# Decay tables made at once, two products on VectorE and a later copy out of PSUM in a fused RWKV and expert-routing kernel

## The chip, the core and the metric

The kernel runs on one core of a Trainium2 chip. A core has five engines with instruction queues of their own: TensorE (PE in the profile; its weight loads are PEld), VectorE (DVE), ScalarE (ACT), GpSimd (POOL) and SyncE (SP), which here only issues DMAs. The metric is the device time of one execution in microseconds. Before the change three runs took 467.05, 468.96 and 474.75 us, median 468.96. Less is better.

## The reference, cut to what matters

```python
# attention: B, H, S, D = 4, 8, 768, 48; everything float32
for t in range(S):
    cur = einsum('bhd,bhe->bhde', u[None] * kt, vt)
    y[:, :, t] = einsum('bhd,bhde->bhe', rt, state + cur)
    state = w[None, :, :, None] * state + einsum('bhd,bhe->bhde', kt, vt)
# bridge: x = y as (B*S, H*D) = (3072, 384) rows
logits = x @ w_gate                       # 8 experts
probs = softmax(logits); expert_idx = argmax(logits)
for e in range(8):                        # F = 1024
    out[mask_e] = gate_w * (relu(x[mask_e] @ w1[e]) @ w2[e])
```

Each head has a decay `w` per channel. In chunks of 128 steps the recurrence becomes matrix products: scores within a chunk (with powers of the decay on both sides, masked to the past), the step's own term r·(u k) on the diagonal, and a state of 48x48 carried from chunk to chunk.

## The kernel before, in words

The attention is cut into 16 units: 4 batches times 4 pairs of heads. The two heads of a pair lie at partitions 0 and 64. A unit has 6 chunks (G) of 128 steps. The loop over `i` (line 509) makes one turn per unit, and one more. Within a turn the program text sets the order on every engine: nothing is reordered, and each engine runs its own queue in that order. Semaphores between engines follow from which tiles an instruction reads and writes; for a PSUM tile they hold by bank, whichever columns are meant.

In a turn i:

- SP issues the load of r and k of unit i+3 (`load_rk`), and near the end that of v and the keys (`load_vk`).
- PE multiplies r·k by u (`p_own`, L258) into the PSUM tile `dsb`. DVE transposes that into `own` (`own_t`, L262). The L258 matmuls are the first of a turn, so their times mark where turns begin.
- PE makes the scores of chunks 0 to 3 into `X0` and `X1` (`p_scores`, L270, 16 passes of the profile), and later those of chunks 4 and 5 into `X23` (L270 again, 8 passes): "the last scores".
- DVE scales r and k of the next unit by the decay table TT (`scale`, L239). POOL waits for `own` by a copy of one element (`turn`, L518), then makes the next unit's r·k (`pairs`, L245) and its decayed keys (`keys`, L249). In four turns `keys` is on DVE.
- ACT writes 12 diagonal blocks of `A` from `own` (`diag`, L276). DVE then copies the masked scores over them: `mask(i, 0)` and `mask(i, 1)` (L282) from X0 and X1, and `mask(i, 2)` (L284), the third mask, from X23.
- PE makes the chunk states into `dsb` (`p_ds`, L293), and DVE scans over them (`scan`, L298).
- PE turns the output of unit i-2 into rows by token (`p_tr`, L331): four chunks into the PSUM tile `tr` and two into `X23`, at columns of the same banks that the last scores use. ACT copies both into the row store `xb` (`keep`, L336 and L337): "the copy of the stored rows".
- PE makes the output of unit i-1 (`p_out`, L313 from A and v, L318 from the state) into `yps`, and ACT copies it out (`out_t`, L323).

Every fourth turn DVE chooses experts for a batch (`choose`), PE ranks the tokens (`p_rank`), and POOL sends rows to DRAM by indirect DMA (`send`, L383). The first units need the tables. `decays(h, n)` (L140 to L144) makes TT for n pairs of heads from pair h on, by one copy and seven doublings; `key_decay` and `p_key_decay` (L147, L152, L153) make the key table T3 by a product on DVE, a transpose on PE and a copy on ACT. Before the loop this is done for pair 0, and in turns 0, 1 and 2 for pairs 1, 2 and 3. `p_fill` (L104) are matmuls whose result nobody reads.

After the loop come nine passes over the experts (`Pass`, L431 for the first layer and L442 for the second). The first pass loads its rows (`first.load`) once the sends of batches 0 to 2 are in DRAM, and transposes them on DVE (`xT`, L423).

Of the kernel before, what the change touches and what calls it, by code (L numbers as in the profile page):

```python
# [21 lines left out]
HP = H // 2  # L22
# [15 lines left out]
def bc(ap, shape):  # L38
    return ap.to_broadcast(shape)


def straight(tc, rk, vk, w, w1, w2, out, flag):
# [8 lines left out]
    nc = tc.nc  # L51
# [33 lines left out]
    def load_rk(i):  # L85
        if i < U:
            b, hp = divmod(i, HP)
            nc.sync.dma_start(rks[i % 3][0:KP], rk[b, hp].rearrange("h p u s -> (h p) u s")[0:KP])
# [12 lines left out]
    def p_fill(n):  # L101

        for _ in range(n):
            nc.tensor.matmul(tr[:, 384:512], lhsT=ident, rhs=ident, start=True, stop=True, skip_group_check=True)  # L104
# [7 lines left out]
        nc.sync.dma_start(rows.rearrange("(e n) c -> e (n c)", e=E)[:, PAD * HP * Q:CAP * HP * Q].rearrange(  # L112
            "e (p z) -> p e z", p=128), bc(zt[:, None, :], [128, E, nz]))

    p_fill(14)
    strict = cp.tile([128, C], FP32, name="strict")
    nc.gpsimd.memset(strict, 1.0)
    nc.gpsimd.affine_select(out=strict, in_=strict, pattern=[[1, C]], base=-1, channel_multiplier=-1,
# [14 lines left out]
    def two(h0, nh, first, second, n):  # L133

        a = TTf[:, h0 * 2 * C + first:h0 * 2 * C + first + n]
        return bass.AP(a.tensor, a.offset, [list(a.ap[0]), [2 * C, nh], [second - first, 2], [1, n]])

    def decays(h0, nh):

        nc.vector.tensor_copy(two(h0, nh, 0, 2 * C - 1, 1), bc(inv[:, h0:h0 + nh, None, None], [KP, nh, 2, 1]))  # L140
        for l in range(7):
            n = 1 << l
            nc.vector.tensor_tensor(two(h0, nh, n, 2 * C - 2 * n, n), two(h0, nh, 0, 2 * C - n, n),  # L143
                                    bc(pw[:, l, h0:h0 + nh, None, None], [KP, nh, 2, n]), op=ALU.mult)  # L144

    def key_decay(h0, nh):
        nc.vector.tensor_tensor(T3c[:, h0:h0 + nh, :], TT[:, h0:h0 + nh, 1, :],  # L147
                                bc(pw[:, 7, h0:h0 + nh, None], [KP, nh, C]), op=ALU.mult)

    def p_key_decay(h0, nh):  # L150
        for hp in range(h0, h0 + nh):
            nc.tensor.transpose(tr[:, hp * 128:hp * 128 + KP], T3c[:, hp, :], ident[0:KP, 0:KP])  # L152
        nc.scalar.copy(T3[:, h0:h0 + nh].rearrange("p a (h d) -> p a h d", h=2),  # L153
                       tr[:, h0 * 128:(h0 + nh) * 128].rearrange("p (a h d) -> p a h d", a=nh, h=2)[:, :, :, 0:D])
# [18 lines left out]
    turn = cp.tile([1, 1], FP32, name="turn")  # L173

    def selection():
        for par in range(2):
            for h in range(2):
                o = 64 * (h ^ par)
                nc.gpsimd.tensor_copy(sel[:, par, :, h * D:(h + 1) * D], bc(ident[0:KP, None, o:o + D], [KP, HP, D]))
        nc.gpsimd.tensor_copy(sel[:, :, :, 2 * D:], wgs)  # L180
# [42 lines left out]
    own = [ca.tile([128, G, 32], FP32, name=f"own{i}") for i in range(2)]  # L223
# [13 lines left out]
    def scale(i):  # L237
        hp, x = i % HP, rks[i % 3]
        nc.vector.tensor_tensor(RKs[i % 3][0:KP].rearrange("p u (c t) -> p u c t", t=C),  # L239
                                x[0:KP].rearrange("p u (c t) -> p u c t", t=C),  # L240
                                bc(TT[:, hp, :, None, :], [KP, 2, G, C]), op=ALU.mult)

    def pairs(i, eng=None):
        x = rks[i % 3]
        (eng or nc.gpsimd).tensor_tensor(rps[i % 2][0:KP], x[0:KP, 0], x[0:KP, 1], op=ALU.mult)  # L245

    def keys(i, eng=None):
        hp, v = i % HP, vks[i % 4]
        (eng or nc.gpsimd).tensor_tensor(Kds[i % 2], v[:, G:2 * G - 1, :], bc(T3[:, hp, None, :], [128, G - 1, 2 * D]),  # L249
                                         op=ALU.mult)  # L250

    def p_own(i):


        hp = i % HP
        x = rps[i % 2][0:KP].rearrange("p (c a j) -> p a c j", a=4, j=32)
        for a in range(4):
            nc.tensor.matmul(dsb[32 * a:32 * a + 2, 240:240 + 32 * G].rearrange("p (c j) -> p c j", j=32),  # L258
                             lhsT=ubs[:, hp, :], rhs=x[:, a], start=True, stop=True, skip_group_check=True)

    def own_t(i):
        nc.vector.transpose(own[i % 2].rearrange("p c m -> p (c m)"), dsb[:, 240:240 + 32 * G])  # L262

    def p_scores(i, cs):
        r = RKs[i % 3]
        for c in cs:
            for h in range(2):
                q = slice(64 * h, 64 * h + D)
                o = X01[h][:, c, :] if c < 4 else X23[:, h, (c - 4) * C:(c - 3) * C]
                nc.tensor.matmul(o, lhsT=r[q, 1, c * C:(c + 1) * C], rhs=r[q, 0, c * C:(c + 1) * C],  # L270
                                 start=True, stop=True, skip_group_check=True)

    def diag(i):
        A = Aw[i % 2]
        for c, h in [(c, 0) for c in range(4)] + [(c, 1) for c in range(4)] + [(c, h) for h in range(2) for c in (4, 5)]:
            nc.scalar.activation(A[:, place(c, h), :], ident, func=ACT.Copy, scale=own[i % 2][:, c, h:h + 1])  # L276

    def mask(i, k):
        A = Aw[i % 2]
        m = strict.bitcast(I32)  # L280
        if k < 2:
            nc.vector.copy_predicated(A[:, 4 * k:4 * k + 4, :], bc(m[:, None, :], [128, 4, C]), X01[k])  # L282
        else:
            nc.vector.copy_predicated(A[:, 8:12, :].rearrange("p (h c) t -> p h c t", h=2),  # L284
                                      bc(m[:, None, None, :], [128, 2, 2, C]),
                                      X23[:, :, 0:2 * C].rearrange("p h (c t) -> p h c t", c=2))

    def p_ds(i):
        v = vks[i % 4]
        d = dsb[:, 0:240].rearrange("p (e g) -> p e g", g=G - 1)  # L290
        for c in range(G - 1):
            for h in range(2):
                nc.tensor.matmul(d[64 * h:64 * h + D, :, c], lhsT=Kds[i % 2][:, c, h * D:(h + 1) * D],  # L293
                                 rhs=v[:, c, h * D:(h + 1) * D], start=True, stop=True, skip_group_check=True)
# [26 lines left out]
    def out_t(i):  # L321
        for k in range(2):
            nc.scalar.copy(yTs[i % 3][0:KP, k], yps[0:KP, k, 0:S // 2])  # L323
# [10 lines left out]
    def keep(i):  # L334
        b, hp = divmod(i, HP)
        nc.scalar.copy(xbs[b % 2][:, 0:4, hp, :], trv[0])  # L336
        nc.scalar.copy(xbs[b % 2][:, 4:G, hp, :], trv[1])  # L337
# [158 lines left out]
        for k, cs in enumerate(((0,), (1, 2), (3, 4), (5,)) if b < B - 2 else ((0, 1), (2, 3, 4, 5))):  # L496
            sends[4 * b + 6 + k] = (b, cs)

    decays(0, 1)
    scale(0)  # L500
    pairs(0, nc.vector)
    key_decay(0, 1)
# [2 lines left out]
    p_own(0)  # L505
    own_t(0)
    p_key_decay(0, 1)
    keys(0)
    for i in range(U + 1):
        last = i == U  # L510
        b, k = divmod(i - 6, 4)
        rt = i >= 6 and k == 0 and b < B - 1
        load_rk(i + 3)
        if not last:
            if i > 0:
                p_own(i)
                own_t(i)
            nc.gpsimd.tensor_copy(turn, own[i % 2][0:1, 0, 0:1])  # L518
            p_scores(i, range(4) if i > 0 else range(2, 4))
            if 0 < i < 3:  # L520
                p_fill(4)
        if i + 1 < U:
            if i + 1 < HP:
                decays(i + 1, 1)
            scale(i + 1)
            if i + 1 < HP:
                key_decay(i + 1, 1)
                p_key_decay(i + 1, 1)
            pairs(i + 1)
            keys(i + 1, nc.vector if i in (7, 8, 11, 12) else None)  # L530
        if i == 0:
            selection()
        if i == 2:
            numbers()
        if not last:
            diag(i)
            mask(i, 0)
            mask(i, 1)
            p_ds(i)
        if rt:  # L540
            p_rank(b)
            slots(b)
        if not last:
            scan(i)
        if 2 <= i:
            p_tr(i - 2)
            keep(i - 2)
        if not last:
            p_scores(i, range(4, G))
            mask(i, 2)  # L550
        if rt:
            gates(b)
            total(b)
            ids(b)
        if i in sends:
            send(*sends[i])
        if 1 <= i:
            p_out(i - 1)
            out_t(i - 1)
        if i % 4 == 1 and i > 4:  # L560
            choose((i - 5) // 4)
        load_vk(i + 3)
        if i == 3:
            clear()
        if i in (12, 13):
            (weights1, weights2)[i - 12](0)
        if i == 14:
            weights1(1)
        if i == U - 1:
            count(cnt3)  # L570
            nc.vector.tensor_scalar(out=viol[:, 12:13], in0=cnt3[:, 0:1], scalar1=float(EARLY), scalar2=None, op0=ALU.is_lt)
            weights2(1, range(2))
            first.load()
            weights2(1, range(2, DT))
# [583 lines left out]
```

## Time and profile before

| | us |
|---|---|
| median of three runs | 468.96 |
| the profiled execution | 470.53 |
| its span, first to last instruction | 468.6 |
| loop over the units, from its first turn but one to the first expert matmul | 21.6 to 185.8 |
| mean of turns 3 to 14 | 10.0 |
| PE busy, share of the span | 421.4, 90% |

A row of the timeline has the start in us, the time from the start of its first to the end of its last instruction, the engine, the line, what is written from what, how many instructions are merged in the row, and in brackets how long the engine was idle before it and what ended that. PE rows count passes: a float32 matmul has two. "Granted clock" is TensorE's, as a share of 2.4 GHz, so 0.50 is 1.2 GHz.

### The profile page before, as it was taken

To read this page: it belongs to the slowest core of one execution; us is meant where nothing else is said; L and a number is where in the kernel's file an instruction comes from. 1 tells how busy PE (TensorE), PEld (TensorE's weight loads), DVE (VectorE), ACT (ScalarE), POOL (GpSimd) and SP (SyncE) were. 2 spreads that over 40 slices of the span, in tenths; PEclk is the share of its full clock that TensorE was granted. 3 is DMA by queue.
4 is the path that set the end of the run, shared out by engine and by line. 5 is a ranking of instruction groups with operands and counts; after the bars stand their busy time and mean duration, and the time that the engine had idled before them with its cause. 6 is when DMAs were issued, how large, how long until landed. Compare 5 with 4: busy or idle time off the path is not lost.

```text
span 468.6 us, 7143 instructions
## 1 busy us (share of the span) xinstructions
PE 421.4 (90%) x2767; PEld 290.9 (62%) x2767; DVE 147.6 (31%) x304; ACT 119.3 (25%) x337; POOL 189.7 (40%) x200
## 2 busy tenths in 40 slices
PE   7386898889788888999999999999999999999992
PEld 6265677668666767877575555555555555455692
DVE  7766445564654642212111111120130120211020
ACT  1334444564644553302202012011011021001200
POOL 3424433465665561133221037046055064076741
PEclk9557757876888888999999999999999999999998
DMA  8902373463445954058584255354273273312401
GB/s 229 254 8 99 107 216 107 139 224 128 149 130 177 375 235 138 18 150 208 148 227 117 84 160 160 93 157 131 90 180 113 90 201 103 104 55 64 139 19 43
DMA packets 33675, 65.22 MB, mean 139 GB/s; under 512 B 17911, under 2 KB 18947, under 8 KB 33632
## 3 DMA queue, kind: packets, MB, share of 16 engines
q1 hardware_dynamic: 28896, 54.83, 40.1%
q0 software_dynamic: 4736, 9.84, 6.2%
q8 instruction: 24, 0.39, 0.4%
q14 instruction: 19, 0.16, 0.1%
HBM read 53.55 MB, written 11.50 MB: 139 GB/s over the span
## 4 chain that ended last, share of the span: by engine, by line
PE 79%; ACT 12%; DVE 3%; issue 1%; POOL 0%; POOLq 0%; DVEq 0%; ACTq 0%
PE X L431 29%; PE yps L442 18%; ACT A L276 9%; PE dsb L442 9%; PE yps L313 8%; PE yps L318 4%; PE X L270 4%; PE dsb L258 2%; DVE TT L143 1%; PE tr L331 1%; PE yps L463 1%; PE dsb L463 1%; ACT xb L336 1%; PE dsb L293 1%; DVE own L262 1%
## 5 line engine op out<-in xcount | busy, mean ns | idle before, releaser
L482 POOL DMA_INDIRECT out_dram<-yo,ix x96 | 94.1, 980 | 158.3 <-DVE yo L479 110.4
L431 PE MATMUL X<-xT,w1s 128*128 128x416 f32 (+2 forms) x432 | 136.2, 475 | 1.3 <-PE yps L442 0.9
L431 PEld LDWEIGHTS X<-xT,w1s 128*128 128x128 f32 x432 | 79.1, 190 | 55.9 <-issue 52.4
L433 ACT ACTIVATE hT<-X 128x416 f32<-128x416 f32 (+2 forms) x72 | 34.5, 479 | 218.9 <-PE X L431 205.8
L442 PE MATMUL yps<-hT,w2s 128*128 128x416 f32 (+2 forms) x288 | 85.8, 451 | 0.7 <-DVE yq L444 0.7
L442 PEld LDWEIGHTS yps<-hT,w2s 128*128 128x128 f32 x288 | 51.4, 190 | 33.0 <-issue 30.9
L276 ACT ACTIVATE A<-ident,own 128x128 f32<-128x128 f32 x192 | 57.9, 388 | 2.8 <-DVE own L262 2.4
L270 PE MATMUL X<-RK 48*128 48x128 f32 x384 | 35.9, 327 | 21.0 <-ACT xb L337 19.8
L444 DVE STREAM_TRANSPOSE yq<-yps 128x416 f32<-128x416 f32 (+2 forms) x18 | 9.7, 537 | 127.8 <-PE yps L442 127.8
L270 PEld LDWEIGHTS X<-RK 48*128 48x128 f32 x384 | 28.6, 218 | 30.7 <-ACT xb L337 22.5
L518 POOL COPY turn<-own 1x1 f32<-1x1 f32 x16 | 21.7, 1359 | 58.2 <-DVE own L262 49.8
L442 PE MATMUL dsb<-hT,w2s 128*128 128x416 f32 (+2 forms) x144 | 42.8, 450 | 0.0
L313 PE MATMUL yps<-A,vk 128*48 128x128 f32 x384 | 37.7, 371 | 0.0
L442 PEld LDWEIGHTS dsb<-hT,w2s 128*128 128x128 f32 x144 | 25.7, 190 | 15.7 <-issue 15.3
L313 PEld LDWEIGHTS yps<-A,vk 128*48 128x48 f32 x384 | 31.0, 168 | 2.6 <-issue 0.9
L383 POOL DMA_INDIRECT rows<-xb,slot x24 | 24.1, 1004 | 20.1 <-DVE osum L379 12.0
L323 ACT COPY yT<-yps 112x384 f32<-112x384 f32 x32 | 13.8, 482 | 67.8 <-PE yps L318 67.8
L423 DVE STREAM_TRANSPOSE xT<-xs 128x416 f32<-128x416 f32 (+2 forms) x27 | 13.1, 535 | 49.0 <-DMA xs<-rows 49.0
L239 DVE TENSOR_TENSOR RK<-rk,TT 112x1536 f32<-112x1536 f32 x16 | 27.6, 1727 | 0.5 <-DMA rk<-in_rk_dram 0.4
L245 POOL TENSOR_TENSOR rp<-rk 112x768 f32<-112x768 f32 x15 | 27.1, 1808 | 0.0
L282 DVE COPY_PREDICATED A<-strict,X 128x512 f32<-128x512 int32 x32 | 23.1, 736 | 10.9 <-ACT A L276 8.8
L249 POOL TENSOR_TENSOR Kd<-vk,T 128x480 f32<-128x480 f32 x12 | 14.3, 1196 | 17.6 <-ACT T L153 17.6
(104 smaller groups left out, 287.5 us busy)
## 6 DMA issues: line engine op xcount, KB each, us to landing
w1s<-in_w_dram SPq DMA_DIRECT2D x40, 384.0 KB, 3.3
w2s<-in_w_dram SPq DMA_DIRECT2D x24, 512.0 KB, 3.5
rk<-in_rk_dram SPq DMA_DIRECT2D x16, 672.0 KB, 5.9
vk<-in_vk_dram SPq DMA_DIRECT2D x16, 528.0 KB, 4.4
xs<-rows SPq DMA_DIRECT2D x28, 169.0 KB, 4.2
out_dram<-yo,ix POOLq DMA_INDIRECT x96, 2.9
rows<-zt SPq DMA_DIRECT2D x1, 1248.0 KB, 7.8
xs<-rows SPq DMA_DIRECT2D x4, 104.0 KB, 2.6
```

The lines of the kernel that those rows point to most:

```text
L239: nc.vector.tensor_tensor(RKs[i % 3][0:KP].rearrange("p u (c t) -> p u c t", t=C), x[0:KP].rearrange("p u (c t) -> p u c t", t=C), bc(TT[: ...
L245: (eng or nc.gpsimd).tensor_tensor(rps[i % 2][0:KP], x[0:KP, 0], x[0:KP, 1], op=ALU.mult)
L270: nc.tensor.matmul(o, lhsT=r[q, 1, c * C:(c + 1) * C], rhs=r[q, 0, c * C:(c + 1) * C], start=True, stop=True, skip_group_check=True)
L276: nc.scalar.activation(A[:, place(c, h), :], ident, func=ACT.Copy, scale=own[i % 2][:, c, h:h + 1])
L282: nc.vector.copy_predicated(A[:, 4 * k:4 * k + 4, :], bc(m[:, None, :], [128, 4, C]), X01[k])
L313: nc.tensor.matmul(o(c, h), lhsT=v[:, c, h * D:(h + 1) * D], rhs=A[:, place(c, h), :], start=c < 2, stop=c == 0, skip_group_check=True)
L383: s_ = nc.gpsimd.indirect_dma_start(out=rows[:, :], out_offset=bass.IndirectOffsetOnAxis(ap=slot[b % 2][:, c:c + 1], axis=0), in_=xbs[b % ...
L431: nc.tensor.matmul(p[:, 0:self.n], lhsT=w1s[self.e % 2][f // 2][:, m, f % 2 * 128:(f % 2 + 1) * 128], rhs=self.t[:, m, 0:self.n], start=m ...
L433: nc.scalar.activation(h[:, f, 0:self.n], p[:, 0:self.n], func=ACT.Relu)
L442: nc.tensor.matmul(p[:, 0:n], lhsT=w2s[self.e % 2][m][:, f, :], rhs=self.h[:, f, 0:n], start=f == 0, stop=f == FT - 1, skip_group_check=True)
L482: s_ = nc.gpsimd.indirect_dma_start(out=out4[:, :], out_offset=bass.IndirectOffsetOnAxis(ap=ix[:, k:k + 1], axis=0), in_=yo[:, k, :], in_o ...
L518: nc.gpsimd.tensor_copy(turn, own[i % 2][0:1, 0, 0:1])
```

## The change

- All four decay tables are made at once ahead of the loop (`decays(0, HP)`), and the key tables of pairs 1 to 3 together in turn 0. Turns 1 and 2 have none of it any more.
- The first unit's `keys` and the second unit's `pairs` run on DVE and no longer on POOL. POOL's one-element copy `turn` is left out in turn 0.
- 17 instead of 14 unread matmuls stand at the start, and the 4 each in turns 1 and 2 are gone.
- In each turn `keep(i-2)` stands behind the last scores and the third mask.
- `numbers` (13 small POOL instructions and two of DVE) moves from turn 2 to 3, and `clear` (zeros for part of the row store) from turn 3 to 4.

```diff
-    p_fill(14)
+    p_fill(17)
...
-    decays(0, 1)
+    decays(0, HP)
     scale(0)
     pairs(0, nc.vector)
     key_decay(0, 1)
...
     p_key_decay(0, 1)
-    keys(0)
     for i in range(U + 1):
...
                 p_own(i)
                 own_t(i)
-            nc.gpsimd.tensor_copy(turn, own[i % 2][0:1, 0, 0:1])
+                nc.gpsimd.tensor_copy(turn, own[i % 2][0:1, 0, 0:1])
             p_scores(i, range(4) if i > 0 else range(2, 4))
-            if 0 < i < 3:
-                p_fill(4)
+        if i == 0:
+            keys(0, nc.vector)
         if i + 1 < U:
-            if i + 1 < HP:
-                decays(i + 1, 1)
             scale(i + 1)
-            if i + 1 < HP:
-                key_decay(i + 1, 1)
-                p_key_decay(i + 1, 1)
-            pairs(i + 1)
-            keys(i + 1, nc.vector if i in (7, 8, 11, 12) else None)
-        if i == 0:
-            selection()
-        if i == 2:
+            if i > 0:
+                pairs(i + 1)
+                keys(i + 1, nc.vector if i in (7, 8, 11, 12) else None)
+            else:
+                pairs(1, nc.vector)
+                key_decay(1, HP - 1)
+                p_key_decay(1, HP - 1)
+                keys(1)
+                selection()
+        if i == 3:
             numbers()
...
         if 2 <= i:
             p_tr(i - 2)
-            keep(i - 2)
         if not last:
             p_scores(i, range(4, G))
             mask(i, 2)
+        if 2 <= i:
+            keep(i - 2)
...
-        if i == 3:
+        if i == 4:
             clear()
```

How the queues stand is shown at three places. First PE in turn 2, from the stored rows of unit 0 (L331) to the outputs of unit 1 (L313, L318) and the next turn's L258; X_69 is X23, and the words in brackets are the engines that an instruction waits for. Before:

```order
L331 MATMUL tr<-sel,yT_179 128x104 [waits Activation_49]
L331 MATMUL tr<-sel,yT_179 128x104 x3
L331 MATMUL X_69<-sel,yT_179 128x104 x2
L270 MATMUL X_69<-RK_168 128x128 [waits Activation_49]
L270 MATMUL X_69<-RK_168 128x128 x3
L313 MATMUL yps<-A_174,vk_85 48x128 x12
L318 MATMUL yps<-RK_167,S_176 48x128 x10
L258 MATMUL dsb<-rp_170,wug 2x192 [waits DVE_49,Pool_49]
```

And with the change:

```order
L331 MATMUL tr<-sel,yT_182 128x104 [waits Activation_49] x2
L331 MATMUL tr<-sel,yT_182 128x104 x2
L331 MATMUL X_69<-sel,yT_182 128x104 x2
L270 MATMUL X_69<-RK_171 128x128 x4
L313 MATMUL yps<-A_177,vk_85 48x128 x12
L318 MATMUL yps<-RK_170,S_179 48x128 x10
L258 MATMUL dsb<-rp_173,wug 2x192 [waits DVE_49,Pool_49]
```

The order of the matmuls is the same; the wait of the last scores for ACT is gone.

Second ACT in turn 2 and at the start of turn 3: the diagonal blocks (L276), the copy of the stored rows (L336, L337) and the copy of an output (L323). Before:

```order
L276 ACTIVATE A_173<-ident,own_177 128x128 [waits DVE_49,Activation_49]
L276 ACTIVATE A_173<-ident,own_177 128x128 [waits Activation_49] x11
L336 COPY xb_182<-tr 128x4x104 [waits PE_49]
L337 COPY xb_182<-X_69 128x2x104 [waits PE_49]
L323 COPY yT_180<-yps 112x384 [waits PE_49]
```

And with the change:

```order
L276 ACTIVATE A_176<-ident,own_180 128x128 [waits DVE_49,Activation_49]
L276 ACTIVATE A_176<-ident,own_180 128x128 [waits Activation_49] x11
L336 COPY xb_185<-tr 128x4x104 [waits PE_49]
L337 COPY xb_185<-X_69 128x2x104 [waits DVE_49]
L323 COPY yT_183<-yps 112x384 [waits PE_49]
```

ACT's order is the same; its second copy (L337) waits for DVE's third mask and no longer for PE alone.

Third DVE from the first transpose of `own` on, in turn 0. Before:

```order
L262 STREAM_TRANSPOSE own_177<-dsb 128x192 [waits PE_49]
L140 COPY TT<-inv 112x2
L143 TENSOR_TENSOR TT<-TT,pw 112x2 [waits DVE_49]
L143 TENSOR_TENSOR TT<-TT,pw 112x2x2 [waits DVE_49]
L143 TENSOR_TENSOR TT<-TT,pw 112x2x4 [waits DVE_49]
L143 TENSOR_TENSOR TT<-TT,pw 112x2x8 [waits DVE_49]
L143 TENSOR_TENSOR TT<-TT,pw 112x2x16 [waits DVE_49]
L143 TENSOR_TENSOR TT<-TT,pw 112x2x32 [waits DVE_49]
L143 TENSOR_TENSOR TT<-TT,pw 112x128 [waits DVE_49]
L239 TENSOR_TENSOR RK_167<-rk_82,TT 112x1536 [waits DMAHW3_49,DVE_49]
L147 TENSOR_TENSOR T3c<-TT,pw 112x128
```

And with the change:

```order
L262 STREAM_TRANSPOSE own_180<-dsb 128x192 [waits PE_49]
L249 TENSOR_TENSOR Kd_174<-vk_84,T_133 128x480 [waits DMAHW2_49,Activation_49]
L239 TENSOR_TENSOR RK_170<-rk_82,TT 112x1536 [waits DMAHW3_49]
L245 TENSOR_TENSOR rp_173<-rk_82 112x768
L147 TENSOR_TENSOR T3c<-TT,pw 112x384
```

The eight table instructions are replaced by `keys(0)` and, behind the scaling, `pairs(1)`; the product for T3 is three times as wide.

## Rows read from the trace of the kernel before

**Rows 1.** The page: PE's busy us and share, and its granted clock in 40 slices.

```profile
PE 421.4 (90%) x2767; PEld 290.9 (62%) x2767; DVE 147.6 (31%) x304; ACT 119.3 (25%) x337; POOL 189.7 (40%) x200
PEclk9557757876888888999999999999999999999998
```

**Rows 2.** The page's costliest groups: busy us, mean ns | idle before, what ended it.

```profile
L270 PE MATMUL X<-RK 48*128 48x128 f32 x384 | 35.9, 327 | 21.0 <-ACT xb L337 19.8
...
L282 DVE COPY_PREDICATED A<-strict,X 128x512 f32<-128x512 int32 x32 | 23.1, 736 | 10.9 <-ACT A L276 8.8
```

**Rows 3.** The timeline, from turn 12's last scores to those of turn 13.

```profile
148.81 0.71 PE L270 MATMUL X<-RK 48*128 48x128 f32 x8 [1.65 <-ACT xb L337]
...
151.74 0.51 PE L258 MATMUL dsb<-rp,wug 112*2 112x192 f32 x8
...
152.38 0.38 DVE L262 STREAM_TRANSPOSE own<-dsb 128x192 f32<-128x192 f32 x1 [1.99 <-PE dsb L258]
...
152.86 3.62 ACT L276 ACTIVATE A<-ident,own 128x128 f32<-128x128 f32 x12 [0.15 <-DVE own L262]
...
154.83 0.61 PE L331 MATMUL X<-sel,yT 112*128 112x104 f32 x4
...
155.97 0.64 DVE L298 TENSOR_TENSOR_SCAN S<-dec,dsb 112x240 f32<-112x240 f32 x1
...
156.78 0.32 ACT L337 COPY xb<-X 128x208 f32<-128x208 f32 x1
157.15 0.80 PE L270 MATMUL X<-RK 48*128 48x128 f32 x8 [1.71 <-ACT xb L337]
```

**Rows 4.** Stretches: length, busy us by engine, then granted clock, DMA share, GB/s.

```profile
57.00:60.80 3.80, 3.80 (x52) 3.05 (x52) 0.73 (x1) 0.00 (x0) 0.52 (x2) 0.72 0.10 14
61.00:72.00 11.00, 10.58 (x92) 8.75 (x88) 4.72 (x6) 5.32 (x16) 4.49 (x3) 0.50 0.73 222
...
144.50:157.00 12.50, 9.29 (x151) 7.81 (x148) 8.63 (x11) 9.23 (x30) 10.01 (x7) 1.00 0.67 222
```

**Rows 5.** The timeline, PE in turn 4 and the start of turn 5.

```profile
60.89 0.82 PE L258 MATMUL dsb<-rp,wug 112*2 112x192 f32 x8
...
64.62 2.04 PE L331 MATMUL tr<-sel,yT 112*128 112x104 f32 x8
...
67.94 1.23 PE L270 MATMUL X<-RK 48*128 48x128 f32 x8 [0.42 <-ACT xb L337]
...
72.84 0.51 PE L258 MATMUL dsb<-rp,wug 112*2 112x192 f32 x8
```

**Rows 6.** The timeline: where turns 1, 2, 3 and 15 begin.

```profile
21.59 0.82 PE L258 MATMUL dsb<-rp,wug 112*2 112x192 f32 x8 [1.93 <-DVE S L298]
...
34.87 0.51 PE L258 MATMUL dsb<-rp,wug 112*2 112x192 f32 x8
...
51.38 0.71 PE L258 MATMUL dsb<-rp,wug 112*2 112x192 f32 x8
...
171.51 0.51 PE L258 MATMUL dsb<-rp,wug 112*2 112x192 f32 x8
```

**Rows 7.** The timeline of the start: DVE's table products, scaling and r·k.

```profile
4.59 2.09 DVE L143 TENSOR_TENSOR TT<-TT,pw 112x2 f32<-112x2 f32 x7
7.05 1.76 DVE L239 TENSOR_TENSOR RK<-rk,TT 112x1536 f32<-112x1536 f32 x1 [0.37 <-DMA rk<-in_rk_dram]
8.73 0.95 DVE L245 TENSOR_TENSOR rp<-rk 112x768 f32<-112x768 f32 x1
...
10.78 4.19 DVE L143 TENSOR_TENSOR TT<-TT,pw 112x2 f32<-112x2 f32 x7
```

**Rows 8.** The timeline from turn 14's last small DVE instruction to the first expert.

```profile
169.29 0.17 DVE L379 TENSOR_TENSOR osum<-osp,osum 128x8 bf16<-128x8 f32 x1
...
184.30 1.10 DVE L423 STREAM_TRANSPOSE xT<-xs 128x256 f32<-128x256 f32 x3 [2.47 <-DMA xs<-rows]
...
185.84 1.56 PE L431 MATMUL X<-xT,w1s 128*128 128x256 f32 x6
```

## The prediction, on record before the run

> **What bounds the kernel now.** I read the page first. PE is busy for 90% of the span, but its granted clock is at full only from the middle on; in the first 40% of the slices it swings between 5 and 9 tenths [rows 1]. So the experts, in the later part of the span, run at the full level of 2.4 GHz, and the turns over the units do not. The groups then say what PE waits for in the turns: of 21.0 us of idle time ahead of the score matmuls, 19.8 ended with ACT's second copy of the stored rows, L337 [rows 2].
>
> The timeline shows why [rows 3]. Turn 13 begins at 151.74. DVE has `own` ready 1.02 later, ACT writes 12 diagonal blocks from 152.86 to 156.48, then makes the two copies, the second until 157.10. Meanwhile PE has gone gapless through L258, L270, L293 and L331 until 155.44, and stands 1.71 us until that copy is done, since the last scores go to its bank. The copy needs nothing from the diagonal; it only stands behind it in ACT's queue. So the chain of such a turn is L258, `own`, 3.62 of diagonal, 0.62 of copies, last scores, outputs, and ACT is the longer half of it.
>
> The clock is the second part of the price. At 57.00 PE starts again after such a wait, and over the next 3.8 us, all of them busy, the clock falls (0.72 on average); from 61 to 72 it is 0.50, which is 1.2 GHz, through PE's whole turn 4 [rows 4]. That turn takes 11.95 us, of which only 0.42 are that wait [rows 5]. Between 144.5 and 157.0 the clock held at 1.00 [rows 4], and there one piece of PE's work, from the last scores at 148.81 to the end of the stored rows at 155.44, holds each group of a turn once without a gap: **6.63 us** [rows 3]. Turns 3 to 14 take 120.13 us together, 10.01 each [rows 6]. They are a mixture of shorter turns with the long wait and of turns near 12 at the low clock.
>
> **The change part by part.** All of it is summed against the profiled execution, 470.53, which lies 1.57 above the median of 468.96.
>
> *Later copy, turns 3 to 14.* The last scores no longer wait for ACT. PE then has the 6.63 of one turn ahead of it, if all it needs comes in time. Measured from a turn's start [rows 3]: the scan ends at 4.87, the diagonal at 4.74, the third mask (0.74, [rows 2]) at about 5.6, the copy behind it at about 6.2, all by 6.63, when the next turn begins. The output's copy on ACT then starts at 6.63 and the next diagonal at 6.63 + 1.12. So PE is the bound, gapless. In three turns the ranking, and in three the choice of experts ahead of `own`, add some 0.2 each (my estimate): 12 x 6.63 + 1.2 = 80.8, against 120.13: **-39.3**. Here I take the clock to stay at full when PE has no gap. The bounds for a turn are 6.63 and 11.53 ([rows 5] without the wait); I take the lower one because the clock held for 12.5 us with one wait of 1.65 in it [rows 3, 4], and where it fell a gap stood before.
>
> The copy's new wait is no accident of this kernel. In the trace matmuls into X23 wait for a read of other columns of the same banks [rows 2]. The Trainium skill (PSUM — Partial Sum Buffer, "PSUM bank collisions raise a hardware error") demands it: two engines are to be kept apart by bank, two readers too. By that rule the wait is not deleted but moved from PE to ACT, behind DVE's third mask; its price is the 0.7 us that stands above in the times of a turn, and it is nil for PE as long as ACT's turn is shorter than PE's.
>
> *Turn 2*, with tables before: 51.38 - 34.87 = 16.51 [rows 6]; now as the others if the clock has risen in turn 1: 6.63, **-9.9**. If not, 11.53 and -5.0.
>
> *Turn 1*: 13.28 [rows 6]. It has no stored rows yet, and I expect it at the low clock, since PE still waits in turn 0. Turn 4 [rows 5] without L331 and the wait (64.62 to 67.94) takes 11.95 - 3.32 = 8.63; L318 at the end of that turn was at full clock already, so about 9.07: **-4.2**. The unread matmuls that go from turns 1 and 2 stood beside the tables, and cost nothing now or then.
>
> *Start.* Between the first `own` and the second unit's scaling, DVE spent 4.38 on tables (0.19 of copy and gaps, 4.19 for seven products, [rows 7]): gone. New on the way to the first diagonal: wider tables ahead of everything, 762 elements more at 1.15 ns (1536 in 1.76, [rows 7]), 0.8 to 0.9, of which 0.37 is covered by DVE's wait for the first r and k: 0.45; `keys(0)` on DVE, 0.6 (480 elements, by the 768 in 0.95 [rows 7]); its wait for T3, 0.2; `pairs(1)` 0.9; T3's product three times as wide, 0.3; two more transposes at the low clock and a wider copy, about 1.0 (estimates). Sum **-1.0**; the bounds are 0 and -2. The three more unread matmuls at the start end before the first scores can begin. `numbers` and `clear` move to turns where POOL and SP have room: nothing.
>
> *End.* Here the gain is partly given back. In the profile 16.0 us pass from the end of turn 14's last small instruction (169.46) to the transposed rows of the first expert (185.40): sends on POOL, then the load. That chain does not shrink with PE. In a short turn the small instruction ends about 7.0 after turn 14's start, so the first expert starts near 23.0; turn 15 begins at 6.8, so 16.2 are left from there, against 185.84 - 171.51 = 14.33 [rows 6, 8]: +1.9. PE has less than two turns of work in those 16.2 (one turn of unit 15, then rows and outputs only), so it stands some 4 to 5 us, and the clock will fall. What that costs the first expert is between 0 and the 7 us that its first layer takes; I take 2.2. **+4.1**.
>
> Sum: -39.3 - 9.9 - 4.2 - 1.0 + 4.1 = -50.3. 470.53 - 50.3 = 420.2, or 418.7 seen from the median. Forecast **419 us**.
>
> **The rivals.**
>
> *The clock still falls in part.* No row shows a whole turn without a gap, so that it holds is inferred. For this rival: from 61 to 72 PE was busy 10.58 of 11.00 and the clock stayed down [rows 4], so eleven us of nearly gapless work can leave it low. Against: no row before shows a fall without a gap ahead of it. If every other turn were at 11.5, twelve turns cost 6 x 4.9 = 29 more: 448.
>
> *Another engine becomes the bound.* ACT's turn is 3.62 of diagonal, 0.62 of copies, the new wait of 0.7 and the output's copies, which I take at under 1: near 5.9. What could lengthen it is DVE and POOL, which stop each other: in the start the seven table products took 4.19 beside two products of POOL, and the same seven 2.09 earlier, beside a short copy [rows 7]. If in short turns POOL's work reaches into the next scaling and holds it for as much as these differ, about 2, the scan ends at 6.9, the third mask at 7.7 and ACT's second copy at 8.1; the output's copy and the next diagonal queue behind it, a turn settles near 7.5, and 12 x 0.9 = 11 more: 430. The Trainium skill (SBUF — State Buffer, "SBUF: two separate sides") states this as a lock held for a whole instruction, against VectorE instructions with two SBUF inputs; the two prices of the products agree with it.
>
> *The last scores wait anyway*, for the third mask of the turn before or the stored rows' bank. Against: PE's order list has no wait there. Only the start and turns 1 and 2 would gain, 1.0 + 4.2 + 6.5 (turn 2 at the mean of 10.0): 457.
>
> *Slower: the clock never rises.* The place is the end of turn 1. Before, gaps and bursts alternated, and the clock came back with the outputs of some turns. If gapless turns at 1.2 GHz leave it there, as 61 to 72 did for eleven us, turn 1 ends at 29.7 and 13 turns of 11.53 bring turn 15 to 179.5 instead of 171.51: +8, and PE at the low level then needs 19 instead of 14.3 to the first expert (11.53, 3.3 of stored rows [rows 5], and about 4.2 of outputs): +5. That is 482. It decides from 10.0 us per turn upward.
>
> **How the numbers follow.** Chances: forecast 0.70, clock falls in part 0.17, another engine 0.06, waits anyway 0.03, slower 0.04. The forecast's own bounds: turn 2 at the low clock (+5) or one late turn more upward, no loss of clock at the end and a start 1 us better downward: 412 to 428. The range reaches up to the second rival and to the milder half of the first, a fall in every third turn at most: **408 to 440**. A measurement of this kernel tells about 2% from no change. Faster by over 2% (below 459.6) are the forecast and the first two rivals: 0.93. Within 2%, where 457 may be read: 0.03. Slower: 0.04.
>
> **What would show it.** In the new profile: no idle time ahead of L270 ended by L337; L258 rows 6.6 to 6.9 apart from turn 2 or 3 on, and a granted clock of 1.00 over them; L337 waiting for L284 on ACT; turn 1 at 20 to 21; a wait of DVE for the first expert's rows of 4 us or more longer than 2.47, PE idle there, and the clock low behind it. L258 rows over 9 apart with the clock at 0.50 would make the forecast wrong by the first or last rival; 7.3 or more apart at full clock, with PE waiting for DVE or ACT, by the second.

## The result, and the profile after

The changed kernel takes **421.38 us** (median of 4 runs, 420.53 to 422.24) against 468.91 (4 runs, 467.05 to 474.75) on the same chip: a ratio of **0.900**, 95% interval 0.896 to 0.903. The forecast was 419 us, the range 408 to 440. The profiled execution takes 422.24, with a span of 420.4 against 468.6, so 48.2 us are to be found.

The page, PE's busy time and its granted clock, to be held against [rows 1]; then three groups with the idle time ahead of them, PE's score matmuls, PE's L258 and ACT's second copy, to be held against [rows 2]:

```profile
PE 393.9 (94%) x2757; PEld 270.7 (64%) x2757; DVE 141.8 (34%) x280; ACT 119.8 (28%) x335; POOL 188.7 (45%) x197
PEclk9679599999999899999999999999999999999997
```

```profile
L270 PE MATMUL X<-RK 48*128 48x128 f32 x384 | 33.2, 309 | 1.3 <-DVE RK L239 1.3
L258 PE MATMUL dsb<-rp,wug 112*2 112x192 f32 x128 | 8.5, 339 | 3.7 <-DVE S L298 3.5 <-DVE rp L245 0.2
L337 ACT COPY xb<-X 128x208 f32<-128x208 f32 x16 | 5.3, 332 | 13.5 <-DVE A L284 11.7 <-DMA rows<-xb,slot 1.7
```

The 19.8 us in which PE waited for ACT's copy are gone. ACT itself now waits 11.7 us ahead of L337, for DVE's third mask: the wait has moved, and PE does not see it. Between the start and the last slice the granted clock falls in two places: in the slice with the 8, from 137 us on, behind the wait for the first expert's rows, which was foreseen, and in the slice with the 5, around 42 to 53 us, which was not.

The timeline of turn 8, one of the undisturbed ones (columns as in [rows 3]):

```profile
73.98 0.51 PE L258 MATMUL dsb<-rp,wug 112*2 112x192 f32 x8
...
75.10 3.62 ACT L276 ACTIVATE A<-ident,own 128x128 f32<-128x128 f32 x12
...
77.61 0.71 PE L270 MATMUL X<-RK 48*128 48x128 f32 x8
...
78.93 0.74 DVE L284 COPY_PREDICATED A<-strict,X 128x512 f32<-128x512 int32 x1
79.70 0.33 ACT L337 COPY xb<-X 128x208 f32<-128x208 f32 x1 [0.59 <-DVE A L284]
79.70 0.90 PE L318 MATMUL yps<-RK,S 48*48 48x128 f32 x20
```

The last scores start at 77.61, while ACT is still busy with its diagonal, and the copy comes 2 us behind them. The next L258 row is at 80.53, 6.55 after this turn began.

Now the exception, turns 3 and 4, first as timeline rows, then as stretches (columns as in [rows 4]):

```profile
34.82 0.51 PE L258 MATMUL dsb<-rp,wug 112*2 112x192 f32 x8
...
35.78 1.72 DVE L239 TENSOR_TENSOR RK<-rk,TT 112x1536 f32<-112x1536 f32 x1
...
37.41 3.45 DVE L198 TENSOR_SCALAR le<-wug 112x4 f32<-112x4 f32 x1
37.49 1.80 POOL L245 TENSOR_TENSOR rp<-rk 112x768 f32<-112x768 f32 x1
...
39.26 1.19 POOL L249 TENSOR_TENSOR Kd<-vk,T 128x480 f32<-128x480 f32 x1
...
40.41 0.28 POOL L183 CAST tri<-strict 128x128 bf16<-128x128 f32 x1
...
40.64 0.19 POOL L184 MEMSET ones<- 128x128 bf16 x1
...
40.98 1.33 DVE L282 COPY_PREDICATED A<-strict,X 128x512 f32<-128x512 int32 x2
...
42.20 0.63 DVE L298 TENSOR_TENSOR_SCAN S<-dec,dsb 112x240 f32<-112x240 f32 x1
...
42.98 0.51 PE L258 MATMUL dsb<-rp,wug 112*2 112x192 f32 x8 [1.54 <-DVE S L298]
```

```profile
43.00:54.00 11.00, 11.00 (x108) 9.23 (x108) 5.22 (x7) 5.32 (x17) 4.93 (x5) 0.55 0.29 78
54.10:120.10 66.00, 66.00 (x1103) 55.39 (x1101) 55.09 (x101) 52.19 (x163) 54.79 (x41) 1.00 0.83 273
131.40:136.70 5.30, 0.00 (x0) 0.00 (x0) 0.43 (x2) 0.86 (x2) 0.00 (x0) 0.95 0.63 169
136.80:141.40 4.60, 4.23 (x18) 3.52 (x18) 0.56 (x2) 1.16 (x3) 0.00 (x0) 0.70 0.02 8
```

`numbers` ends with two instructions of DVE on 112x4 elements. The first, L198, takes 3.45 us. It starts with POOL's r.k product, goes on through its keys, and ends when POOL has come to a memset. The two masks and the scan stand behind it in DVE's queue, PE's next L258 waits for that scan, and after 1.54 us of idle PE the clock is at 0.55 through the whole of turn 4, although PE is busy in every moment of it. From 54.10 to 120.10 PE then has no gap, and the clock no fall.

The end, against [rows 8]: DVE waits for the first expert's rows, PE behind it. In the last two of the stretches above PE is idle for 5.30 us, and behind that the clock is at 0.70.

```profile
113.45 0.51 PE L258 MATMUL dsb<-rp,wug 112*2 112x192 f32 x8
...
120.18 0.51 PE L258 MATMUL dsb<-rp,wug 112*2 112x192 f32 x8
...
136.27 1.10 DVE L423 STREAM_TRANSPOSE xT<-xs 128x256 f32<-128x256 f32 x3 [8.96 <-DMA xs<-rows]
136.77 2.21 PEld L431 LDWEIGHTS X<-xT,w1s 128*128 128x128 f32 x6 [5.59 <-DVE xT L423]
136.77 2.92 PE L431 MATMUL X<-xT,w1s 128*128 128x256 f32 x6 [5.38 <-DVE xT L423]
```

### The profile page after: what moved, and what is told of

Same layout as the page of the kernel before. It is cut to its first block, busy times and chain, and to the rows that moved or that the text cites. A ratio compares the mean times of both kernels' runs of the same rounds, so it can differ in the third digit from the quotient of the medians.

```text
span 420.4 us, 7088 instructions
## 1 busy us (share of the span) xinstructions
PE 393.9 (94%) x2757; PEld 270.7 (64%) x2757; DVE 141.8 (34%) x280; ACT 119.8 (28%) x335; POOL 188.7 (45%) x197
## 4 chain that ended last, share of the span: by engine, by line
PE 87%; DVE 3%; DMA 2%; ACT 1%; issue 1%; POOL 1%; SPq 0%; POOLq 0%; DVEq 0%; ACTq 0%
PE X L431 32%; PE yps L442 20%; PE dsb L442 10%; PE X L270 6%; PE yps L313 5%; PE tr L331 3%; PE yps L318 3%; PE dsb L293 2%; PE dsb L258 2%; PE X L331 1%; PE yps L463 1%; PE dsb L463 1%; DMA rows<-xb,slot 1%; ACT A L276 1%; DVE le L198 1%
## 5 line engine op out<-in xcount | busy, mean ns | idle before, releaser
L431 PE MATMUL X<-xT,w1s 128*128 128x416 f32 (+2 forms) x432 | 137.6, 478 | 6.4 <-DVE xT L423 5.4
L431 PEld LDWEIGHTS X<-xT,w1s 128*128 128x128 f32 x432 | 79.9, 192 | 61.4 <-issue 52.2
L276 ACT ACTIVATE A<-ident,own 128x128 f32<-128x128 f32 x192 | 57.9, 390 | 4.0 <-DVE own L262 2.9
L383 POOL DMA_INDIRECT rows<-xb,slot x24 | 29.6, 1233 | 16.4 <-DVE osum L379 9.7
L270 PE MATMUL X<-RK 48*128 48x128 f32 x384 | 33.2, 309 | 1.3 <-DVE RK L239 1.3
L270 PEld LDWEIGHTS X<-RK 48*128 48x128 f32 x384 | 26.3, 203 | 8.6 <-issue 5.5
L517 POOL COPY turn<-own 1x1 f32<-1x1 f32 x15 | 18.2, 1216 | 19.5 <-DVE own L262 19.4
L313 PE MATMUL yps<-A,vk 128*48 128x128 f32 x384 | 26.4, 291 | 0.0
L245 POOL TENSOR_TENSOR rp<-rk 112x768 f32<-112x768 f32 x14 | 25.4, 1813 | 0.0
L313 PEld LDWEIGHTS yps<-A,vk 128*48 128x48 f32 x384 | 22.1, 131 | 2.2 <-ACT A L276 0.2
L331 PE MATMUL tr<-sel,yT 112*128 112x104 f32 x128 | 19.2, 294 | 0.5 <-ACT yT L323 0.5
L249 POOL TENSOR_TENSOR Kd<-vk,T 128x480 f32<-128x480 f32 x11 | 13.2, 1199 | 11.5 <-ACT T L153 11.5
```

The source lines that it names most:

```text
L313: nc.tensor.matmul(o(c, h), lhsT=v[:, c, h * D:(h + 1) * D], rhs=A[:, place(c, h), :], start=c < 2, stop=c == 0, skip_group_check=True)
L331: nc.tensor.matmul(trv[c // 4][:, c % 4, :], lhsT=yTs[i % 3][0:KP, c & 1, (c // 2) * C:(c // 2 + 1) * C], rhs=sel[:, c & 1, i % HP, :], st ...
L383: s_ = nc.gpsimd.indirect_dma_start(out=rows[:, :], out_offset=bass.IndirectOffsetOnAxis(ap=slot[b % 2][:, c:c + 1], axis=0), in_=xbs[b % ...
L431: nc.tensor.matmul(p[:, 0:self.n], lhsT=w1s[self.e % 2][f // 2][:, m, f % 2 * 128:(f % 2 + 1) * 128], rhs=self.t[:, m, 0:self.n], start=m ...
```

## The experiments

They ran in three sets of four, each set on one chip with runs of the kernel before. Beside the first result all kernels are slower there: before 477.29, 478.36 and 474.68, the changed kernel 432.91 and 432.13. The traces of all twelve have a pause of PE of 3.4 to 5.5 us in the last expert, and those with the copy moved also shorter ones in turns 8 to 10 and 12 to 15, mostly with nothing that the profile shows PE to wait for. So times are compared within a set, and turns by their L258 rows. The kernel before has a trace on the first chip only; where turns are held against [rows 6], it is that one. "Stretches" below are three numbers: where turn 3 starts, how long turns 3 to 14 take, and the time from turn 15's start to the first expert.

**The copy alone** (first set).

```diff
@@ the kernel before
             p_tr(i - 2)
-            keep(i - 2)
         if not last:
             p_scores(i, range(4, G))
             mask(i, 2)
+        if 2 <= i:
+            keep(i - 2)
```

> The kernel before with one edit: the copy of the stored rows behind the last scores and the third mask. Theory (the copy's place carries the gain, tables and start the rest): turns 3 to 14 fall from 120 to 79.5 to 85 us, turns 1 and 2 keep their tables (13.3 and at most 16.5), the end gives 2 to 4 back, so 428 to 438 us. Rival A (the start and the tables are needed, because the clock must be up before turn 3): it stays low for several turns and the time is 445 to 460. Rival B (the copy's place does little): above 460.

Measured: 443.9 us (441.25 to 444.53), ratio to before 0.931 (0.923 to 0.939). The whole change has 0.900 on the first chip and 0.910 and 0.911 on two others (below), so the copy alone carries about 7 of its 9 to 10%. Stretches: 49.26, 83.24, 18.9. Turns 1 and 2 are 13.31 and 14.78. In the fourth kernel of this set, which has the whole change and no long L198, turns 3 to 14 take 83.24 as well: in them the rest of the change adds nothing. The new start and tables are not needed for that (rival A): with the old ones the clock is at 1.00 too from turn 3's start to 132.40, and PE has no idle time that ACT's copy ended:

```profile
L270 PE MATMUL X<-RK 48*128 48x128 f32 x384 | 33.1, 306 | 0.9 <-DVE RK L239 0.9
```

The time is 6 us above the upper end expected; the pauses make more than that, about 4 in six turns that take 7.1 to 7.4 instead of 6.55, and 5.5 in the last expert.

**All but the copy** (first set): the changed kernel, `keep` back between `p_tr` and the last scores.

```diff
             p_tr(i - 2)
+            keep(i - 2)
...
             mask(i, 2)
-        if 2 <= i:
-            keep(i - 2)
```

> The changed kernel with the copy of the stored rows put back ahead of the last scores; tables, start, numbers and the unread matmuls as changed. Theory: ACT's second copy again ends PE's wait in every turn, about 1.7 us at full clock, and the clock falls again in some; the start and turns 1 and 2 gain 5 to 12, so 455 to 465. Rival A (the start holds the clock up for all later turns): 12 turns of 8.3 instead of 10.0, so 435 to 445. Rival B (the rest does nothing): 468.

Measured: 465.19 us (464.68 to 465.61), 0.977 (0.969 to 0.984), 0.2 above the theory's upper end. The stretches are 38.38, 113.60, 21.2. PE's wait for ACT is back, longer in sum than before (the group of L270):

```profile
L270 PE MATMUL X<-RK 48*128 48x128 f32 x384 | 33.4, 310 | 29.2 <-ACT xb L337 26.9 <-DVE RK L239 2.4
```

Turns are 8.6 to 9.9, so the clock falls in some, whatever the start did (rival A falls). The start and turns 1 and 2 gain 11 to 13 us by turn 3's start (against 49.26 above and 51.38 in [rows 6]); at the end some of it is lost again. Turns 3 to 14 take 6.5 less than in [rows 6], though the wait is in them, for none is near 12; why is not shown.

**The wait filled, not removed** (first set). Seven unread matmuls in PE's wait; the copy stays where it was.

```diff
@@ the kernel before
             p_tr(i - 2)
             keep(i - 2)
+            if not last:
+                y_fill(7)   # 128x128 into yps, which the outputs overwrite
```

> The kernel before with seven unread 128x128 matmuls into the output's bank between the stored rows and the last scores of turns 2 to 15: about 1.5 us at full clock, in PE's wait for ACT, which stays. Theory (two prices, the wait and the clock that falls behind it): the turns stay near 8.3 at full clock, 12 x 8.3 = 100 against 120, so 445 to 455. Rival (only the wait counts, the clock falls for another reason): 465 to 490, the unread matmuls lengthening each slow turn by up to 3 us.

Measured: 460.75 us (460.46 to 463.11), 0.967 (0.959 to 0.974). Turn 8, from its timeline:

```profile
85.99 0.51 PE L258 MATMUL dsb<-rp,wug 112*2 112x192 f32 x8
...
89.53 1.75 PE L501 MATMUL yps<-ident 128*128 128x128 f32 x14
...
91.03 0.32 ACT L337 COPY xb<-X 128x208 f32<-128x208 f32 x1
...
91.40 0.71 PE L270 MATMUL X<-RK 48*128 48x128 f32 x8
...
94.32 0.51 PE L258 MATMUL dsb<-rp,wug 112*2 112x192 f32 x8
```

The last scores still stand behind ACT's copy, only PE is busy until then. The granted clock stays up:

```profile
52.70:152.70 100.00, 98.77 (x1487) 85.13 (x1485) 65.78 (x115) 61.53 (x195) 64.44 (x48) 1.00 0.67 220
```

Every turn from 3 to 14 takes 8.33 to 8.41, 100.06 together where the kernel before took 120.13 [rows 6]. With the same wait at full clock 20 us are gone. So the wait had two prices of about equal size: itself, 12 times 1.7, and the low clock behind it, another 20. The experiment shows it without moving anything. The total is 6 us above the range expected: the end gives 4.9 back (19.2 against 14.33), and the pause in the last expert is 4.8.

**The two small instructions in turn 15** (first set, again in the third).

```diff
@@ numbers(), its last two instructions (L198, L199)
+    def in_range():
         nc.vector.tensor_scalar(out=le, in0=wt, ...)
         nc.vector.scalar_tensor_tensor(out=okw, in0=wt, ...)
...
         if i == U - 1:
+            in_range()
             count(cnt3)
```

> The changed kernel with the two small DVE instructions of numbers (the test of the decay rates, 112x4) moved from turn 3 to turn 15; POOL's part of numbers stays in turn 3. Theory (the first of the two is held for 3.45 us beside POOL's r.k and keys, which makes PE wait 1.54 and drops the clock through turn 4): turns 3 and 4 become 6.6 each, 1.6 + 4.5 = 6 us less, 414 to 417. Rival A (DVE is held by POOL's fourteen small instructions, and the masks would have been): 420 to 422. Rival B (another wait drops the clock in turn 4): 418 to 421.

Measured: 429.09 us (428.7 to 429.53), 0.900 (0.894 to 0.907). Its turns 3 and 4 are 6.55 and 6.56 where they were 8.16 and 11.07. The mechanism is as expected; the total could not be read against a run of the changed kernel, which this set lacked.

```profile
35.12 0.51 PE L258 MATMUL dsb<-rp,wug 112*2 112x192 f32 x8
...
41.67 0.51 PE L258 MATMUL dsb<-rp,wug 112*2 112x192 f32 x8
...
48.23 0.51 PE L258 MATMUL dsb<-rp,wug 112*2 112x192 f32 x8
...
128.70 0.15 DVE L198 TENSOR_SCALAR le<-wug 112x4 f32<-112x4 f32 x1
```

> The changed kernel a third time, as the measure for the run with the two DVE instructions in turn 15 on the same chip: 421 to 422 if this chip shows no pauses of PE, 431 to 434 if it shows them as in the second set.

> The changed kernel with the two small DVE instructions of numbers in turn 15, beside the changed kernel on one chip. Theory (the first of them, held for 3.45 us, makes turns 3 and 4 take 19.2 instead of 13.1): 4 to 6 us less than the changed kernel, 1.0 to 1.4%. Rival (PE then only waits longer for the first expert's rows at the end, since the sends on POOL set that): 0 to 2 less; but those sends start with turn 15 too, so they should come earlier by the same.

Measured on one chip: 432.13 us (431.02 to 432.9) with the instructions in turn 3, 429.35 (428.52 to 429.85) with them in turn 15. All four runs of the one lie below all four of the other: 2.8 us or 0.65% less, between theory and rival. The profile of the slower shows why it is not 6. L198 again takes 3.32, PE again stands 1.42 ahead of turn 4, but this time the clock stays up:

```profile
35.30:43.30 8.00, 6.62 (x110) 5.48 (x108) 7.32 (x8) 4.87 (x15) 6.45 (x17) 1.00 0.67 198
43.40:49.80 6.40, 6.40 (x108) 5.42 (x107) 5.10 (x7) 5.31 (x17) 5.06 (x5) 1.00 0.43 139
```

So in the five executions profiled with L198 in turn 3 it costs 1.4 to 1.6 us of idle PE, and 4.3 to 4.5 more in turn 4 in the three where the clock falls behind it. The 2.8 us are not its price alone: of the 2.5 us between these two profiled executions 1.5 are turn 3, and 1.3 lie behind the first expert's start, where the two kernels are the same.

**What holds the instruction** (third set, one run). Three more instructions of that size in the kernel above, results unread.

```diff
+        if i == 4:   # SBUF to SBUF, one input
+            nc.vector.tensor_scalar(out=spare[:, 0, :], in0=wt, scalar1=W_HI, scalar2=None, op0=ALU.is_le)
+        if i == 5:   # input in PSUM
+            nc.vector.tensor_scalar(out=spare[:, 1, :], in0=X01[0][0:KP, 0, 0:HP], ...)
+        if i == 9:   # two inputs in SBUF
+            nc.vector.scalar_tensor_tensor(out=spare[:, 2, :], in0=wt, scalar=W_LO, in1=wt, ...)
```

> The same kernel with three more 112x4 instructions of DVE behind the scaling, whose results nobody reads: in turn 4 the one that was held (one input, SBUF to SBUF), in turn 5 the same with its input in PSUM, in turn 9 one with two inputs in SBUF, of the form of the other small instruction. Theory (an instruction of DVE that needs what POOL's r.k and keys hold waits until POOL lets go; from PSUM it needs nothing of that): 3 to 3.5 us in turn 4 with the next turn 1.5 late, 0.15 to 0.2 in turn 5, and turn 9 as turn 4 if two inputs need it too. Rival (turn 3 was an accident of numbers' own instructions on POOL): 0.2 in all three.

The timeline around each (turn 4, turn 5, turn 9):

```profile
42.33 1.52 POOL L194 CAST pos<-it 128x13 f32<-128x13 int32 x1
...
43.71 0.16 DVE L536 TENSOR_SCALAR spare<-wug 112x4 f32<-112x4 f32 x1
...
43.79 0.14 POOL L195 IOTA it<- 128x4 int32 x1
...
50.26 0.15 DVE L538 TENSOR_SCALAR spare<-X 112x4 f32<-112x4 f32 x1
...
50.34 1.82 POOL L245 TENSOR_TENSOR rp<-rk 112x768 f32<-112x768 f32 x1
...
78.79 3.09 DVE L540 SCALAR_TENSOR_TENSOR spare<-wug 112x4 f32<-112x4 f32 x1
...
78.88 1.81 POOL L245 TENSOR_TENSOR rp<-rk 112x768 f32<-112x768 f32 x1
...
80.66 1.20 POOL L249 TENSOR_TENSOR Kd<-vk,T 128x480 f32<-128x480 f32 x1
...
83.80 0.51 PE L258 MATMUL dsb<-rp,wug 112*2 112x192 f32 x8 [1.42 <-DVE S L298]
```

Two of the three came out as the theory has it. In turn 9 the instruction is held for 3.09 us, through POOL's r.k and keys. Turn 9 takes 8.88 instead of the 7.40 of the same kernel without it, and turn 10, at a clock of 0.56, takes 11.69 instead of 7.22. Together that is 5.9 us more; the time, 434.03 in its one run, is 4.7 above. The one whose input lies in PSUM starts just as shortly before POOL's r.k and takes 0.15. The one in turn 4 was a miss: 0.16. POOL was late in that turn, still in `numbers`' own small instructions, and went on to an iota, which reads nothing. So it is not the instruction's kind alone; what POOL starts at that moment counts too. In the kernel before, where the same L198 took 0.16, POOL was idle, 3.96 us in all:

```profile
41.13 0.16 DVE L198 TENSOR_SCALAR le<-wug 112x4 f32<-112x4 f32 x1
...
41.93 1.20 POOL L249 TENSOR_TENSOR Kd<-vk,T 128x480 f32<-128x480 f32 x1 [3.96 <-ACT T L153]
```

The Trainium skill (SBUF — State Buffer, "SBUF: two separate sides") speaks of a lock on a port pair that VectorE and GpSimd share; whichever starts first has it for a whole instruction, and the other waits that out fully. The trace agrees that the loser waits out whole instructions. It differs in two points: L198 was held over two of POOL's instructions in a row (1.80 and 1.19), and it was the one held although its row begins 0.08 us ahead of POOL's. The Trainium skill names for it, in the same section, VectorE instructions with two SBUF inputs and those in a 2-port mode. L198 has one input, and no run shows its mode. That an instruction with its input in PSUM goes free rests on a single row.

**The end** (second set, and one in the third). In the first result PE stands 5.4 us ahead of the first expert. Three kernels of the second set put work there.

> The changed kernel once more, as the measure for the three runs beside it. If the pauses of PE that the profile puts down to issue in the first four experiments (0.3 to 0.9 us in some turns, 4 to 5.5 in the last expert) belong to the chip and its moment and not to the edits, it shows them too when this chip does: 428 to 431 then, else 421 to 422. Rival (the edits moved the code so that PE is starved): 421 to 422 here whatever the others show.

```diff
-    first.xT()
-    first.L1(range(0, 1))
     p_tr(U - 1)
     keep(U - 1)
     choose(B - 1)
+    first.xT()
+    first.L1(range(0, 1))
```

> The changed kernel with the stored rows of unit 15, their copy and the last choice ahead of the first expert's rows and matmuls. Theory (PE has no work in 5.4 us at the first expert, and the 2.4 us of L331 behind it can go there): 2.4 us less than the changed kernel, up to 4 if the clock then holds. Rival (the choice's six DVE instructions, about 1.9 us, delay the transposed rows): 0 to 1 less.

```diff
+    p_fill(20)
     first.xT()
```

> The changed kernel with 20 unread 128x128 matmuls (about 4.3 us at full clock) on PE ahead of the first expert, in the 5.4 us in which it stands. Theory (the clock falls behind that wait and the first six matmuls of the expert take 2.92 instead of 1.56): 1.4 to 2 us less. Rival (the fall has another cause, or the wait ends sooner than the filling): 0 to 1 us more.

```diff
@@ the kernel with the two instructions in turn 15
-    first.xT()
-    first.L1(range(0, 1))
     p_tr(U - 1)
+    for _ in range(9):   # unread, 128x128 into yps
+        nc.tensor.matmul(yps[:, 0, 0:128], lhsT=ident, rhs=ident, ...)
     keep(U - 1)
     choose(B - 1)
+    first.xT()
+    first.L1(range(0, 1))
```

> Both cures on the changed kernel: the two small DVE instructions in turn 15, the stored rows of unit 15 and the choice ahead of the first expert, and 9 unread matmuls into the output's bank behind those rows. Theory: 6 (turns 3 and 4) + 2.4 (rows) + 1.4 (clock) = 10 less than the changed kernel. Rival (the sends on POOL, not PE, set when the first expert can start, so that what turns 3 and 4 gain is kept but the end gives nothing): 6 less. Rival B (the held instruction is not the cause of turns 3 and 4): 0 to 4 less.

Measured: the changed kernel 432.91 (431.58 to 434.56), the rows of unit 15 first 438.59 (436.82 to 439.92), the filling 437.04 (435.0 to 438.93), both cures 431.88 (431.29 to 433.02). None of these answers the question, because in the changed kernel on this chip PE has no wait there. Its outputs of turn 15 come in pieces; two of them, in the changed kernel run again, and its pause in the last expert:

```profile
129.35 0.41 PE L313 MATMUL yps<-A,vk 128*48 128x128 f32 x3 [0.29 <-issue]
...
130.77 0.45 PE L313 MATMUL yps<-A,vk 128*48 128x128 f32 x4 [0.43 <-issue]
...
397.36 7.01 PE L431 MATMUL X<-xT,w1s 128*128 128x416 f32 x12 [4.13 <-ACT hT L433]
```

These 24 matmuls last from 128.42 to 134.73 instead of 1.52 us, the expert's rows are there first, and whatever is put ahead of the expert comes on top: from turn 15's start it begins after 19.34 us in the changed kernel, 24.2 with rows and choice ahead (there xT stands behind the choice's six instructions, as the rival had it), 23.4 with the filling, 24.55 with rows, choice and nine matmuls. The last kernel's gain in turns 3 and 4 pays for that loss. The expectation that the pauses belong to chip and moment and not to the edits holds: the changed kernel itself shows them, at 432.91, 2 us above the range expected for that case. What they are stays open.

```diff
@@ the kernel with the two instructions in turn 15
+    p_tr(U - 1)
+    keep(U - 1)
     first.xT()
     first.L1(range(0, 1))
-    p_tr(U - 1)
-    keep(U - 1)
     choose(B - 1)
```

> The kernel with the two small instructions in turn 15, and the stored rows of unit 15 with their copy ahead of the first expert's matmuls; the choice stays behind them. Theory: where PE stands for 5 us at the first expert, 2 to 4 less than without it; where it has no such wait, 0 to 1 more, for the output's copy on ACT then stands in PE's way (0.6 us).

Measured: 428.24 us (427.9 to 430.79) against 429.35 beside it, ranges that overlap: no difference shown. PE goes without a gap into the first expert in the kernel beside it too, the case for which 0 to 1 more was expected. Of the kernels run, the one with the two instructions in turn 15 is the best that is told apart from the change, by 2.8 us on one chip.

## Why the prediction was right, point by point

The sum against the profiled executions, each term by the L258 and L431 rows of both traces:

| term | predicted | measured |
|---|---|---|
| start, to turn 1 | -1.0 | 21.59 to 20.24: -1.35 |
| turn 1 | -4.2 | 13.28 to 8.03: -5.25 |
| turn 2 | -9.9 | 16.51 to 6.55: -9.96 |
| turns 3 to 14 | -39.3 | 120.13 to 85.36: -34.77 |
| turn 15 to the first expert | +1.9 | 14.33 to 16.59: +2.26 |
| first expert and later | +2.2 | 282.76 to 283.63: +0.87 |
| sum | -50.3 | -48.2 |

That the sums lie only 2.1 apart is in part luck: turns 3 and 4 lost 6.1 us that no term has, turn 15 gave back 0.4 more than forecast, and the other terms together were 4.4 better.

- *PE is bound by the wait and the clock behind it.* Shown by the filled wait: 20 us are the clock, 20 the wait.
- *The copy's wait moves to ACT and costs PE nothing.* Right: ACT waits 0.4 to 0.8 us ahead of L337 in the undisturbed turns, where 0.7 was priced, and 3.55 and 2.32 for the copies of turns 3 and 4, 11.7 in all for DVE's mask; the 1.3 us of idle PE ahead of L270 are all in DVE's scaling. The trace agrees with what the prediction took from the Trainium skill (PSUM — Partial Sum Buffer, "PSUM bank collisions raise a hardware error"): the copy of X23 waits until the mask has read the same banks.
- *A gapless turn of 6.63 at full clock.* Right for ten of twelve: turns 5 to 14 take 66.13 together, 6.61 each. The small surcharge fell only on the three turns in which PE ranks (6, 10 and 14, 6.72 to 6.75). One reason given for the lower bound was misread: in the 12.5 us in which the clock held [rows 4] PE had not one wait but two, 3.2 us in all (12.50 less 9.29 busy). So a wait alone did not bring the clock down there either.
- *Turn 1 at the low clock.* Right; the clock came back within it, in its outputs, a little earlier than taken.
- ***`numbers` and `clear` "cost nothing".*** This is the term that was mis-sized: turns 3 to 14 gave -34.8 where they would have given about -40.9 (120.13 - 79.23, without what turns 3 and 4 have above 6.55 each). `clear` did cost nothing: with it in turn 4 and no L198 ahead, that turn takes 6.56. Of `numbers` I counted only that POOL has room in turn 3. Its last two instructions run on DVE, ahead of that turn's masks, and beside POOL's r.k and keys; there the first takes 3.45 instead of 0.16, PE stands 1.54, and the clock fell: 1.6 + 4.5 us. The rival of DVE and POOL stopping each other had the mechanism, at 0.06, but looked for it in the scaling, in every turn; it came once, in an instruction of four elements. And the rival of a clock that still falls in part happened, in one turn of twelve.
- *The end.* The two halves were mis-sized against each other: PE stood 5.38 and the first six matmuls took 2.92 instead of 1.56, but all behind the first expert's start cost 0.87 and not 2.2. The forecast's own lower bound of 412 does not follow from its two terms, 2.2 and 1 below 419. Whether filling that wait would keep the clock is not shown; no chip of the later sets had the wait.
- *The start.* Right in sum. With tables and start as before, turn 3 begins at 49.26 instead of 35.12 (first set): 1.3 of that is the start, 4.6 turn 1, 8.2 turn 2.

## What to carry to other kernels

A wait of a clocked engine can cost twice; filling it with unread work tells the two prices apart without moving anything. When instructions move, price each on the engine where it runs, beside what the other engines do in its new place: a few elements of DVE beside POOL's products were held for 3.45 us here, and PE stood 1.54 behind them. And count what stands behind them in their queue, since that, not their own time, is what reaches the bound.

## What was not expected of the hardware

- The clock does not answer the same gap in the same way. Behind waits of 1.54, 1.55 and 1.44 ahead of turn 4 it fell (0.55 to 0.56 over about 11 us, PE without a gap); behind 1.42 and 1.55 in the same place of two other executions of the same program up to there it stayed at 1.00, and behind 1.42 ahead of turn 10, in the kernel with the three added instructions, it fell again (11.69 for that turn). In the three executions in which it fell the clock had come back earlier in turn 1, and turn 2 began at 28.06 to 28.27; in the two others it began at 28.74 and 28.92. Whether the moment of the gap decides is not shown.
- Gapless work alone does not bring it back at once: in 43.00 to 54.00 PE is busy for 11.00 of 11.00 us at 0.55, and it is back at 54.10.
- POOL is held by DVE too: its copy of one element (L517) takes 1.36 to 2.12 us beside DVE's scaling, mostly 1.54 to 1.62, and 0.17 to 0.18 in the four turns where it runs behind the scaling (78.06 in turn 8).
